# Stage B of a spectral mixer moved to 64x64 array tiles and the stages around it re-spaced, beside a dense feed-forward network

## Chip, cores, metric

One core of one Trainium2 chip. The metric is the device time of one execution in microseconds (us); lower is better. Every time below is the median of several executions, and all executions that are compared ran in the same (fast) state. "Granted clock" is the share of full TensorE clock that the profile's records show. The profiles are those of one execution each.

## The reference

```python
# x: (8, 3008, 256); filt_r, filt_i: (1505, 256); float32
X = np.fft.rfft(x, axis=1)
y = np.fft.irfft(X * (filt_r + 1j * filt_i)[None], n=3008, axis=1)
t = y.reshape(8 * 3008, 256)                       # 24064 tokens
out = (np.maximum(t @ w_gate, 0) * (t @ w_val)) @ w_out    # 256 -> 1536 -> 256
```

## The kernel before

A Fourier transform of length 3008 = 94 x 32 is done as matmuls. For each of the 8 batches there are these stages, which then feed the network (FFN):

- Stage A: transform of length 94. For batches 2 to 7 it goes in four *chunks* (j = 0 to 3): a load into one of three `XP` buffers, a *fold* of six operations on GpSimd, and a group of 16 small tiles on TensorE (`psF`). The result goes to DRAM (`Abuf`) and comes back as `at`.
- Stage B: transform of length 32 (`psX`), product with the filter on VectorE (`tt`, `uu`), inverse (`psD`). It goes to DRAM (`Dbuf`) and comes back as `dC`.
- Stage C: inverse of length 94 (`psY`), which gives the FFN's input `yT`.
- FFN: 47 blocks of 512 tokens with 12 *steps* each. A step is two `psV`, two `psG` and four `psO` matmuls. The stages of the next batches are hung on fixed step numbers between them, and TensorE takes everything in program order.

Stage A's chunks, and the schedule (cut):

```python
    def load_chunk(b, j):
        xp = XP[(4 * b + j) % 3]
        ...                       # six DMAs, issued by SyncE
    def fold_chunk(b, j):
        ...                       # six tensor_tensor on nc.gpsimd
    def tiled_a(b, j):
        ...                       # 16 tiles of 24 x 32 into four PSUM banks, two copies to asf by
        ...                       # ScalarE and two by VectorE, four DMAs to Abuf
    # the schedule, in FFN steps
        end = (b * S // W - 1) * NFT + C_AT[0] - 5
        sb0 = 19 if b == 1 else end - 30 | 1
        ...
            for j, (l, e) in enumerate(((-66, -41), (-60, -33), (-54, -27), (-40, -17))):
                at_step(sb0 + l, lambda b=b, j=j: load_chunk(b, j))
                at_step(sb0 + l + 1, lambda b=b, j=j: fold_chunk(b, j))
                at_step(sb0 + e, lambda b=b, j=j: tiled_a(b, j))
            at_step(sb0 + e + 4, lambda b=b: load_at_tiled(b))
        for i, f in enumerate(items_b(b)):
            at_step(sb0 + 2 * i, f)
        at_step(sb0 + 27, lambda b=b: load_d(b))
```

Stage B, one pair of groups (cut): each 128x128 matrix holds two 64x64 blocks on its diagonal.

```python
            for i in range(2):
                nc.tensor.matmul(psX[:, i], F2[:, g + i, :], at[:, g + i, :], start=True, stop=True)
            ...
            for i in range(2):
                nc.tensor.matmul(psD[:, i], I2t[:, g + i, :], tt[:, i], start=True, stop=False)
                nc.tensor.matmul(psD[:, i], I2u[:, g + i, :], uu[:, i], start=False, stop=True)
```

## Time and profile before

| | before |
|---|---|
| median, 3 runs before the prediction | 914.12 us (913.38 to 915.36) |
| span of the profiled execution | 911.3 us |
| TensorE busy | 98% |
| FFN starts at (first `psV` of the FFN) | 61.9 us |
| stage B between FFN steps, batches 1 to 7 | 55.0 us of TensorE |
| six fourth-chunk tile groups of stage A, each from the start of the last `psO` before it to the next `psV` | 1.46 us each |

The prediction shows the busy shares, the chain and the stage-B groups. From the page, the granted clock in 40 slices of the span (each digit is tenths; 9 is 90% or more). There is one dip, in the second slice:

```profile
PEclk9899999999999999999999999999999999999999
```

Columns are start (us), length (us), engine, line, operation, output<-input, count.

### The profile page before, as it was taken

To read this page: it belongs to the slowest core of one execution; us is meant where nothing else is said; L and a number is where in the kernel's file an instruction comes from. 1 tells how busy PE (TensorE), PEld (TensorE's weight loads), DVE (VectorE), ACT (ScalarE), POOL (GpSimd) and SP (SyncE) were. 2 spreads that over 40 slices of the span, in tenths; PEclk is the share of its full clock that TensorE was granted. 3 is DMA by queue.
4 is the path that set the end of the run, shared out by engine and by line. 5 is a ranking of instruction groups with operands and counts; after the bars stand their busy time and mean duration, and the time that the engine had idled before them with its cause. 6 is when DMAs were issued, how large, how long until landed. Compare 5 with 4: busy or idle time off the path is not lost.

```text
span 911.3 us, 18044 instructions
## 1 busy us (share of the span) xinstructions
PE 896.0 (98%) x6602; PEld 545.7 (60%) x6602; DVE 578.0 (63%) x875; ACT 500.8 (55%) x893; POOL 262.4 (29%) x181
## 2 busy tenths in 40 slices
PE   8799999999999999999999999999999999999997
PEld 3445665666655666556655566556665566666665
DVE  3737766568655775657755587555865567655553
ACT  4675555555555555555555555555555555555552
POOL 4340174405451074400844017440355300000000
PEclk9899999999999999999999999999999999999999
DMA  9996336444355345452353433525446242231111
GB/s 254 256 252 143 116 122 166 111 90 138 122 153 105 82 150 139 119 117 84 129 168 94 115 111 118 165 76 121 115 134 166 65 106 66 85 78 36 36 31 51
DMA packets 106138, 109.04 MB, mean 120 GB/s; under 512 B 9794, under 2 KB 87362, under 8 KB 105410
## 3 DMA queue, kind: packets, MB, share of 16 engines
q1 hardware_dynamic: 101222, 103.77, 40.7%
q0 software_dynamic: 4512, 3.90, 2.8%
q8 instruction: 52, 0.85, 0.4%
q14 instruction: 36, 0.29, 0.1%
q10 hardware_dynamic: 316, 0.22, 0.1%
HBM read 61.94 MB, written 49.81 MB: 123 GB/s over the span
## 4 chain that ended last, share of the span: by engine, by line
PE 95%; DMA 3%; SPq 0%; ACT 0%; POOL 0%; DVE 0%; issue 0%; ACTq 0%; POOLq 0%
PE psV L445 27%; PE psG L445 27%; PE psO L464 26%; PE psF L321 3%; PE psA L275 3%; PE psY L429 2%; PE psD L383 2%; PE psD L384 2%; PE psX L364 2%; DMA XF<-in_x_dram 1%; DMA Abuf<-asb 1%; DMA at<-Abuf 0%; DMA out_dram<-osb 0%; SPq L178 0%; SPq L478 0%
## 5 line engine op out<-in xcount | busy, mean ns | idle before, releaser
L450 DVE SCALAR_TENSOR_TENSOR prod<-psG,vsb 128x512 bf16<-128x512 f32 x564 | 390.0, 692 | 274.6 <-ACT vsb L448 265.6
L448 ACT CAST vsb<-psV 128x512 bf16<-128x512 f32 x564 | 332.0, 589 | 244.7 <-PE psV L445 206.4
L445 PE MATMUL psV<-yT,WvT 128*128 128x512 bf16 x1128 | 335.9, 379 | 0.9 <-ACT yT L434 0.7
L464 PE MATMUL psO<-WoT,prod 128*128 128x256 bf16 x2256 | 336.4, 273 | 0.0
L445 PE MATMUL psG<-yT,WgT 128*128 128x512 bf16 x1128 | 335.3, 379 | 0.0
L464 PEld LDWEIGHTS <-prod 128*128 128x128 bf16 x2256 | 220.7, 98 | 143.4
L445 PEld LDWEIGHTS <-WgT 128*128 128x128 bf16 x1128 | 110.0, 98 | 133.8 <-issue 0.5
L307 POOL TENSOR_TENSOR fold<-XP 128x1024 f32<-128x1024 f32 x24 | 56.4, 2351 | 404.5 <-DMA out_dram<-osb 170.9
L445 PEld LDWEIGHTS <-WvT 128*128 128x128 bf16 x1128 | 102.3, 98 | 33.1 <-issue 20.9
L386 ACT CAST dsb<-psD 128x512 bf16<-128x512 f32 x96 | 55.9, 588 | 51.7 <-PE psD L384 50.0
L367 DVE TENSOR_TENSOR tt<-psX,Ftr 128x512 bf16<-128x512 f32 x96 | 65.2, 682 | 4.2 <-PE psX L364 4.2
L470 ACT COPY osb<-psO 128x512 f32<-128x512 f32 x92 | 53.9, 586 | 22.7 <-PE psO L464 20.3
L373 DVE TENSOR_TENSOR uu<-psX,Fti 128x512 bf16<-128x512 f32 x90 | 61.3, 681 | 0.0
L308 POOL TENSOR_TENSOR XP<-XP 128x1024 f32<-128x1024 f32 x24 | 56.4, 2349 | 1.9
L384 PE MATMUL psD<-uu,I2u 128*128 128x256 bf16 x192 | 47.6, 276 | 0.6 <-POOL uu L371 0.6
L383 PE MATMUL psD<-tt,I2t 128*128 128x256 bf16 x192 | 47.9, 276 | 0.0
L328 ACT CAST asb<-psF 128x512 bf16<-128x512 f32 x48 | 25.8, 589 | 32.5 <-PE psF L321 32.5
L328 DVE CAST asb<-psF 128x512 bf16<-128x512 f32 x48 | 30.9, 686 | 17.3 <-PE psF L321 14.5
L364 PE MATMUL psX<-at,F 128*128 128x256 bf16 x192 | 37.8, 281 | 3.9 <-DMA at<-Abuf 3.9
L436 DVE CAST yT<-psY 128x512 bf16<-128x512 f32 x47 | 32.0, 681 | 12.9 <-PE psY L429 12.9
L434 ACT CAST yT<-psY 128x512 bf16<-128x512 f32 x47 | 27.5, 586 | 22.7 <-PE psY L429 22.6
L429 PE MATMUL psY<-M,dC 96*128 96x94 bf16 (+18 forms) x604 | 37.5, 198 | 0.0
(64 smaller groups left out, 439.9 us busy)
## 6 DMA issues: line engine op xcount, KB each, us to landing
dC<-Dbuf SPq DMA_DIRECT2D x64, 192.0 KB
XP<-in_x_dram SPq DMA_DIRECT2D x48, 256.0 KB
Dbuf<-dsb SPq DMA_DIRECT2D x31, 384.0 KB
XP<-in_x_dram SPq DMA_DIRECT2D x96, 96.0 KB
Abuf<-asb SPq DMA_DIRECT2D x96, 96.0 KB
at<-Abuf SPq DMA_DIRECT2D x48, 192.0 KB
out_dram<-osb SPq DMA_DIRECT2D x70, 94.0 KB
XF<-in_x_dram SPq DMA_DIRECT2D x12, 256.0 KB
```

Source lines behind the costliest of these rows:

```text
L307: tt(t, xp[:, 0:2], xp[:, 2:4], op=ALU.add)
L308: tt(xp[:, 2:4], xp[:, 0:2], xp[:, 2:4], op=ALU.subtract)
L328: copy(asf[:, :, q, :], banks[q])
L364: nc.tensor.matmul(psX[:, i], F2[:, g + i, :], at[:, g + i, :], start=True, stop=True)
L367: nc.vector.tensor_tensor(tt, psX, Ftr[:, g:g + 2, :], op=ALU.mult)
L373: nc.vector.tensor_tensor(uu, psX, Fti[:, g:g + 2, :], op=ALU.mult)
L383: nc.tensor.matmul(psD[:, i], I2t[:, g + i, :], tt[:, i], start=True, stop=False)
L384: nc.tensor.matmul(psD[:, i], I2u[:, g + i, :], uu[:, i], start=False, stop=True)
L445: nc.tensor.matmul(pt[:, :W], w[:, h, ft * 128:(ft + 1) * 128], yt[:, h, :], start=(h == 0), stop=(h == 1))
L448: nc.scalar.copy(vsb, psV[:, :W])
L450: nc.vector.scalar_tensor_tensor(prod, in0=psG[:, :W], scalar=0.0, in1=vsb, op0=ALU.max, op1=ALU.mult)
L464: nc.tensor.matmul(psO[:, t % 2], prods[ft][:, t * 128:(t + 1) * 128], WoT[:, ft, :], start=(ft == 0), stop=(ft == NFT - 1))
```

## The change

The intent: in a 128x128 matrix with two 64x64 blocks half of the array multiplies by zeros. On 64x64 tiles four blocks run side by side, so stage B's streaming time should halve. To pay for fewer mode switches, inverse and forward pieces are put into one excursion of 24 tile matmuls over four PSUM banks (two of `psX`, and `psv` and `psg` for `psD`), and the products go one to a step. The schedule is re-spaced for that. (Not shown in the cut: for batches 2 to 7 `at` comes in four loads instead of eight, and for batches 1 to 7 stage B's result goes to `Dbuf` in three stores instead of four.) Cut to its core:

```diff
+    def fwd(b, i, es=(0, 1)):
+        ...
+        for m in range(2):
+            for e in es:
+                for a in range(2):
+                    j = 12 * a + 2 * i + m
+                    nc.tensor.matmul(psXs[b, i, e][64 * a:64 * a + 64, m],
+                                     F2[64 * e:64 * e + 64, j, :],
+                                     ats[b][64 * e:64 * e + 64, j, :], start=True, stop=True,
+                                     tile_position=(64 * e, 64 * a))
+    def inv(b, i, tags=None, cuts=CUTS):
+        ...     # 16 matmuls with tile_position=(64 * a, 64 * e), into two banks
     def load_d(b, z0=0, z1=NZ):
         for z in range(z0, z1):
-            nc.sync.dma_start(dC, ...)                       # 96 rows
+            for e in range(2):
+                nc.sync.dma_start(dC[48 * e:48 * e + 48], ...)   # twice 48 rows
 # schedule
         if b == 1:
-                at_step(5, lambda c=c: load_at(1, c))
+                at_step(3, lambda c=c: load_at(1, c))
         else:
-            for j, (l, e) in enumerate(((-66, -41), (-60, -33), (-54, -27), (-40, -17))):
-                at_step(sb0 + l, ...)                        # sb0 = end - 30 | 1
+            for j, (l, e) in enumerate(((-104, -74), (-98, -69), (-92, -62), (-73, -57))):
+                at_step(end + l, ...)
-        for i, f in enumerate(items_b(b)):
-            at_step(sb0 + 2 * i, f)
-        at_step(sb0 + 27, lambda b=b: load_d(b))
+        for i, l in enumerate((-40, -35, -28, -23, -16, -11, -4)):
+            if i < 6:
+                at_step(end + l, lambda b=b, i=i: fwd(b, i))
+                for h in range(4):
+                    at_step(end + l + h, lambda b=b, i=i, h=h: product(b, i, h // 2, h % 2))
+            if i > 0:
+                at_step(end + l, lambda b=b, i=i: inv(b, i - 1, ("psv", "psg")))
+        at_step(end - 2, lambda b=b: load_d(b))
```

In the prologue (batch 0) the forward tiles run one bank at a time, with a filler matmul of 128 columns between them, as before; the forward matrices come by DMA instead of being placed by VectorE.

## The prediction

> **What bounds the kernel now.** I read the page's busy shares first, then the chain that ended last, then the TensorE timeline, and only then the waits.
>
> ```profile
> PE 896.0 (98%) x6602; PEld 545.7 (60%) x6602; DVE 578.0 (63%) x875; ACT 500.8 (55%) x893; POOL 262.4 (29%) x181
> PE 95%; DMA 3%; SPq 0%; ACT 0%; POOL 0%; DVE 0%; issue 0%; ACTq 0%; POOLq 0%
> L384 PE MATMUL psD<-uu,I2u 128*128 128x256 bf16 x192 | 47.6, 276 | 0.6 <-POOL uu L371 0.6
> L383 PE MATMUL psD<-tt,I2t 128*128 128x256 bf16 x192 | 47.9, 276 | 0.0
> L364 PE MATMUL psX<-at,F 128*128 128x256 bf16 x192 | 37.8, 281 | 3.9 <-DMA at<-Abuf 3.9
> ```
>
> TensorE is 95% of the chain, so the time is the sum of what TensorE issues, plus its few waits. VectorE and ScalarE have 37% and 45% to spare on average. The three stage-B groups have no idle before them except 3.9 and 0.6 us, both in the prologue. But their "busy" columns overstate: durations are latencies of overlapping matmuls. The true price is the distance from one start to the next:
>
> ```profile
> 83.11 0.60 PE L464 MATMUL psO<-WoT,prod 128*128 128x256 bf16 x4
> 83.54 0.38 PE L364 MATMUL psX<-at,F 128*128 128x256 bf16 x2
> 83.76 0.59 PE L445 MATMUL psV<-yT,WvT 128*128 128x512 bf16 x2
> 84.19 0.59 PE L445 MATMUL psG<-yT,WgT 128*128 128x512 bf16 x2
> 84.62 0.60 PE L464 MATMUL psO<-WoT,prod 128*128 128x256 bf16 x4
> 85.06 0.41 PE L429 MATMUL psY<-M,dC 96*128 96x10 bf16 x7
> ```
>
> Four 256-column matmuls take 83.54 - 83.11 = 0.43 us, so 0.109 us each; two of 512 columns take 0.43, so 0.216 each. An FFN step is 85.06 - 83.76 = 1.30 us. A batch's stage B is 24 forward and 48 inverse matmuls: 72 x 0.109 = 7.85 us. Seven of the eight batches run it between FFN steps (55 us); batch 0 runs it in the prologue.
>
> Is there a price for array tiles already in this kernel? Yes: the tiled stage A.
>
> ```profile
> 135.37 0.60 PE L464 MATMUL psO<-WoT,prod 128*128 128x256 bf16 x4
> 135.90 0.61 PE L321 MATMUL psF<-XP,WF 24*32 24x512 f32 x1
> ...
> 136.64 0.59 PE L321 MATMUL psF<-XP,WF 24*32 24x512 f32 x1
> 137.16 0.60 PE L445 MATMUL psV<-yT,WvT 128*128 128x512 bf16 x2
> ```
>
> The four psO should hand over at 135.37 + 0.43 = 135.80; the first tile starts at 135.90: entry costs about 0.09 us. The last tile matmul starts at 136.64 and streams 0.43 us (the fp32 psA matmuls follow one another by 0.43), so exit costs 0.52 - 0.43 = 0.09. Tiles of one row group start 7 ns apart, so they do run beside each other.
>
> **What the Trainium skill says.** "TensorEngine Tiling (Array Packing)", Key Properties: changing the tiling mode drains TensorE. The trace agrees: 0.09 us in and 0.09 out. The same page, Restrictions: column tiling turns fast weight load off. "TensorE: Matmul & The Clock Gate", LDWEIGHTS, gives columns / 1.2 ns for a weight load; for 64 columns an estimate of 53 ns. In psF, tiles' two passes start 0.43 or 0.45 us apart, which fits a later weight load (32 columns, 27 ns by that formula) mostly hidden behind the stream; no trace here has a 64-column one. The same page, the clock gate's two states: half clock after an idle window of about 3.4 us. The trace agrees: TensorE was idle from about 29.2 to 33.4 us in the prologue, and the mean granted clock was 0.52 from 31.5 to 38.5 us. I return to this below.
>
> **The change, part by part.**
> 1. Removed: 72 full-array matmuls per batch. They hold two 64x64 blocks on the diagonal and zeros beside them.
> 2. Added: 144 quarter-array matmuls of 256 columns per batch, in 36 quartets. If four tiles run beside each other, a quartet takes 0.109: 36 x 0.109 = 3.92 us. Four weight loads of 53 ns per quartet fit even if two by two they follow one another (0.106).
> 3. Added: mode switches. Before, forward and inverse pieces stood in the normal mode, no switch. Now there are seven excursions per batch: one forward only (2 quartets), five with forward and inverse (6), one inverse only (4). Each costs 0.09 in, 0.09 out and one exposed first weight load, 0.05: 0.23 us (an estimate). Seven: 1.6 us.
> 4. Sum per batch: 7.85 - (3.92 + 1.6) = 2.3 us; allowing 0.02 us stagger per excursion, 2.15. Times 7: 15 us.
> 5. VectorE and ScalarE do the same products (682 ns) and copies (588 ns) as before; they move. One product per step on four successive steps: VectorE needs 0.69 + 0.68 = 1.37 us per step against TensorE's 1.30. Four such steps fall behind by 0.28 us, but each excursion gives TensorE about 0.9 us more to do, and PSUM has two banks for each of psV and psG. The worst place is an excursion on step 11 of a block, where ScalarE queues osb (0.59), two psD copies (1.18) and then the next vsb (0.59). Counting from that block step's start: psD ready at about 2.4, vsb done at 4.1, prod at 4.8, while the psG bank is wanted by the step after next at about 5.2. It holds, with 0.3 to 0.4 us to spare; I book nothing.
> 6. Moved: batch 1's stage B starts at FFN step 11 instead of 19. This is the part I expect to cost time. What it needs is the load of its "at" tile:
>
> ```profile
> 61.40 0.30 SPq L280 DMA_DIRECT2D Abuf<-asb  x1
> 61.74 1.14 SPq L407 DMA_DIRECT2D dC<-Dbuf  x2
> 63.04 9.54 SPq L350 DMA_DIRECT2D at<-Abuf  x4
> 72.64 3.19 SPq L407 DMA_DIRECT2D dC<-Dbuf  x4
> ```
>
> The four loads (384 KB each) are issued until 72.6, and the issue of the last is drawn out: the queue is full. The DMA share is 1.19 from 72 to 76 us and 1.16 from 76 to 80, then 0.09. The queue still carries 512-byte packets until 80; counted in order behind the two dC loads (768 packets), the 3072 at packets end near 76.7, so the tile is usable at about 77. Before, the first forward matmul came at 83.54, 6 us later: no wait. In the changed kernel the loads are requested two steps earlier, but the order of the DMA queue in the built program is the same (two chunks of dC, at, four chunks of dC) and the bandwidth, not the request, limits it. Step 11's side work begins at about 72.3 (the step-12 psV starts at 72.73 in the old trace). So TensorE, which takes instructions in order, should wait about 4.6 us, once.
> 7. That wait is longer than 3.4 us, so it may cover a whole idle window and drop the clock to one half for some microseconds. If the windows run free, a 4.6 us gap covers one with chance (4.6 - 3.4) / 3.4 = 0.35, and then costs 2 to 3 us more (in the prologue half clock lasted 5 us after work resumed). On average 0.9 us.
> 8. Prologue: forward matrices now come by DMA, without the two VectorE placements (1.15 us busy), which lay beside loads. At its end, stage B gains perhaps 0.7 us on TensorE, but the first dC chunks landed near 60.0, when psY started at 60.6, so at most 0.5 shows. I book -0.4.
>
> Sum: 914.1 - 15.0 + 4.6 + 0.9 - 0.4 = 904.2; since the most likely single outcome has no clock drop, I say 903.5 us, -1.2%.
>
> **Rivals.** (a) No wait at step 11, because the loads land earlier than I count. For: the requests are two steps earlier and a half-microsecond shorter prologue helps. Against: the saturated queue until 80 us. It would make 898 to 899 us. (b) Free or nearly free switches, with weights fully hidden: 36 quartets only, a saving of 27 us and, with the wait, about 891. Against: the measured 0.09 each way in stage A. (c) Quartets limited by weight loads or by issue: if the four loads of 53 ns follow one another, a quartet takes 0.21 and the tiles save nothing; stage B would then cost 36 x 0.21 + 1.6 = 9.2 us, and the time would be about 928. Against: psF's sixteen tiles were issued 7 ns apart per row group. (d) VectorE becomes the bound in the four product steps: some 0.3 us for each of 42 product groups at worst, +10 us, 913. For: 1.37 against 1.30. Against: the ledger in point 5, and the 17.9 us that TensorE needs for twelve such steps against VectorE's 14.4 (12 x 0.69 + 0.68 + 8 x 0.68).
>
> **Range and chances.** The saving per batch is known to about 0.4 us (entry weight load and stagger), so 3 us over seven; the wait to 1.5; the clock drop is 0 or 2 to 3; (d) in part perhaps 3. Together 897 to 909. Faster by over 2% means below 895.8, which needs (a) and switches cheaper than measured: 0.1. Slower by over 2% needs (c) in full: 0.02. Within 2%: 0.88.
>
> **What would show it.** Right: no psX or psD group in the normal mode; start-to-start of the quartets near 0.109; from the start of the last psO before a full excursion to the next psV about 1.0 us (0.109 + 0.9); a TensorE wait of 4 to 5 us for "DMA at<-Abuf" near 72 us and none other of its kind; no new TensorE waits for ScalarE or VectorE. Wrong: excursions of 1.2 us or more (then (c)), psV or psG waiting for VectorE in steps after an excursion (then (d)), no wait near 72 us (then (a)).

## More of the kernel before

Now the fourth chunk of batch 2, in three timelines.

SyncE's issues first: the loads of `dC`, and later the first four of the six `XP` loads.

```profile
135.70 4.82 SPq L407 DMA_DIRECT2D dC<-Dbuf  x8
...
147.90 2.69 SPq L294 DMA_DIRECT2D XP<-in_x_dram  x4
```

The fold on GpSimd, its first and its last operation:

```profile
160.34 2.35 POOL L307 TENSOR_TENSOR fold<-XP 128x1024 f32<-128x1024 f32 x1 [12.77 <-DMA out_dram<-osb]
...
169.23 1.26 POOL L312 TENSOR_TENSOR XP<-XP 128x512 f32<-128x512 f32 x1
```

And TensorE, which uses it:

```profile
172.18 0.61 PE L321 MATMUL psF<-XP,WF 24*32 24x512 f32 x1
```

From the first request (147.90) to the end of the fold (169.23 + 1.26 = 170.49) are 22.6 us, and TensorE comes for it at 172.18. So this chain has only 1.7 us of slack in batch 2 (read in the same way, batches 3 to 7 have 3.5 to 6.8 us), and no view of TensorE's waits shows it, since a chain that is just in time makes no wait.

## The result, and the profile after

The changed kernel took 980.55 us (979.04 to 981.17, 4 runs) against 913.88 us (913.38 to 915.36, 4 runs) for the kernel before in the same rounds: ratio 1.072, interval 1.071 to 1.074. It is 7% slower. All ratios here are the mean time of one kernel's fast runs over that of the other's of the same rounds, so they are not quite the ratio of the medians quoted. The mean granted clock fell from 0.995 to 0.956.

From the page of the changed kernel: busy shares, granted clock, chain, and the stage-A tile group (count | busy us, mean ns | idle before, releaser).

```profile
PE 922.8 (94%) x7202; PEld 520.1 (53%) x7202; DVE 567.2 (58%) x873; ACT 497.9 (51%) x890; POOL 262.1 (27%) x181
...
PEclk9698999799998999989998999979999899999999
...
PE 87%; DMA 5%; POOL 4%; SPq 2%; issue 0%; ACT 0%; DVE 0%; POOLq 0%
...
L320 PE MATMUL psF<-XP,WF 24*32 24x512 f32 x384 | 47.5, 708 | 35.4 <-POOL XP L308 35.4
```

TensorE lost four points of busy share, and the chain now runs through DMA, GpSimd and SyncE for 11% of the span (3% before, almost all DMA). The clock line has eight dips instead of one. And the costly wait is at stage A's tiles, whose code the change did not touch. TensorE's waits (total us, times, longest):

```profile
PE psF L320 <- POOL XP L308: 35.4, 6, 7.9
PE psX L361 <- DMA at<-Abuf: 10.6, 2, 6.1
```

Six times, once for each of batches 2 to 7, TensorE waits for a fold. Here is batch 2 again, in the same three views. SyncE:

```profile
145.18 8.66 SPq L422 DMA_DIRECT2D dC<-Dbuf  x16
...
155.62 1.56 SPq L293 DMA_DIRECT2D XP<-in_x_dram  x4
```

GpSimd:

```profile
166.86 2.34 POOL L306 TENSOR_TENSOR fold<-XP 128x1024 f32<-128x1024 f32 x1 [14.27 <-DMA out_dram<-osb]
...
175.71 1.26 POOL L311 TENSOR_TENSOR XP<-XP 128x512 f32<-128x512 f32 x1
```

(The releaser in brackets is inferred. What the fold reads is the loads issued from 155.62 us on.) TensorE, with the idle time before and its releaser in brackets:

```profile
166.86 0.60 PE L480 MATMUL psO<-WoT,prod 128*128 128x256 bf16 x4
173.01 1.91 PE L320 MATMUL psF<-XP,WF 24*32 24x512 f32 x2 [5.55 <-POOL XP L308]
174.35 3.25 PE L320 MATMUL psF<-fold,WF 24*32 24x512 f32 x4
177.03 1.13 PE L320 MATMUL psF<-XP,WF 24*32 24x512 f32 x2
```

At this place the changed kernel is some 8 us behind on the clock (the FFN starts later, and batch 1 costs a wait, see below), so intervals have to be compared, not clock times. From the step that asks for the load to the first tile were 35.0 us before (137.16, that step's first `psV`, to 172.18). Now they would be 25.4 (141.99 to 167.4: the last `psO` starts at 167.19, and 0.11 of stream and 0.09 of entry follow). The request goes out 13.6 us after its step's start instead of 10.7, and from the request to the end of the fold are 21.4 us instead of 22.6. So the fold, which ended 1.7 us before TensorE could use it, now ends 9.6 us after (176.97). Over the six batches it is 7.8 to 11.9 us late. TensorE first waits 5.5 us for the fold's third operation, which gives the first of the four parts. Then the group itself stretches from 173.01 to 177.03 while the other parts come one by one from GpSimd. While TensorE was idle its clock was halved, from 172.63 for 10.24 us. The next `psV` came at 179.28, so the passage from the last `psO`'s start took 12.09 us against 1.46 before. The six fourth groups took 12.1, 12.3, 13.1, 12.4, 14.5 and 10.3 us. That is 65.9 us over 6 x 1.46. Of each half-clock stretch another 1.7 to 3.6 us lie behind the group, where the FFN runs at half speed: 16 us in sum, of which half, 8 us, is lost.

Stage B itself, from the same TensorE timeline, a full excursion in batch 1:

```profile
90.88 0.60 PE L480 MATMUL psO<-WoT,prod 128*128 128x256 bf16 x4
91.41 0.41 PE L361 MATMUL psX<-at,F 64*64 64x256 bf16 x8
91.66 0.28 PE L390 MATMUL psD<-tt,I2t 64*64 64x256 bf16 x4
91.77 0.28 PE L390 MATMUL psD<-uu,I2u 64*64 64x256 bf16 x4
...
92.19 0.60 PE L461 MATMUL psV<-yT,WvT 128*128 128x512 bf16 x2
```

The quartets of `psD` start 0.109 us apart. The last `psO` of four starts at 90.88 + 3 x 0.109 = 91.21, so entry costs 91.41 - 91.21 - 0.109 = 0.09, and the whole excursion adds 92.19 - 91.21 - 0.109 = 0.87 us. Over the trace the 35 full excursions have a median of 0.875, the seven forward-only ones 0.438, the seven inverse-only ones 0.657. A batch costs 5 x 0.875 + 0.438 + 0.657 = 5.47 us where it cost 7.86.

At batch 1, the foreseen wait:

```profile
75.12 0.59 PE L461 MATMUL psG<-yT,WgT 128*128 128x512 bf16 x2
81.86 0.64 PE L361 MATMUL psX<-at,F 64*64 64x256 bf16 x8 [6.14 <-DMA at<-Abuf]
```

The clock was at half from 80.47 for 6.83 us, until 87.30. The excursion took 6.88 us of TensorE instead of 0.44, and of the FFN behind it, from 82.43, 4.9 us ran at half clock: this cost 6.4 + 2.4 = 8.9 us (rounded after adding).

In the prologue, half clock lasted from 32.68 to 49.75 (17.07 us), against 31.75 to 38.58 (6.83 us) before, and the FFN starts at 64.24 instead of 61.91 us. This 2.3 us is uncertain: in the six profiles that have this prologue (this one and those of experiments 2, 3, 5, 8 and the first of 6) the FFN starts between 62.7 and 66.1 us, in the two with the old prologue at 61.9 and 62.9. One stretch of the changed kernel (us; then for PE, PEld, DVE, ACT and POOL busy time and count; granted clock; DMA share; GB/s) shows what is odd in it:

```profile
35.40:38.80 3.40, 3.40 (x34) 1.68 (x32) 3.40 (x7) 1.64 (x3) 1.04 (x1) 0.50 0.65 143
```

TensorE is busy all the time and its clock stays at half. (The profile models the ends of matmuls. By their columns, at the 0.43 us that 512 of them take at half clock, I estimate that something streams for 2.5 to 2.8 of each 3.4 us here.)

The account against the span of before, 979.2 - 911.3 = +67.9 us: fourth tile groups with the half clock after them +73.9, batch 1 +8.9, prologue +2.3, tiles 7 x (5.47 - 7.86) = -16.7. The sum is +68.4, 0.5 us over.

### The profile page after: what moved, and what is told of

Same layout as the page of the kernel before. It is cut to its first block, busy times and chain, and to the rows that moved or that the text cites. A ratio compares the mean times of both kernels' runs of the same rounds, so it can differ in the third digit from the quotient of the medians.

```text
span 979.2 us, 19294 instructions
## 1 busy us (share of the span) xinstructions
PE 922.8 (94%) x7202; PEld 520.1 (53%) x7202; DVE 567.2 (58%) x873; ACT 497.9 (51%) x890; POOL 262.1 (27%) x181
## 4 chain that ended last, share of the span: by engine, by line
PE 87%; DMA 5%; POOL 4%; SPq 2%; issue 0%; ACT 0%; DVE 0%; POOLq 0%
PE psV L461 24%; PE psO L480 24%; PE psG L461 23%; PE psF L320 5%; PE psA L274 3%; PE psD L390 2%; PE psY L445 2%; PE psX L361 2%; POOL XP L307 1%; POOL fold L306 1%; DMA at<-Abuf 1%; DMA out_dram<-osb 1%; DMA Abuf<-asb 1%; SPq L494 1%; DMA XP<-in_x_dram 1%; POOL XP L308 1%
## 5 line engine op out<-in xcount | busy, mean ns | idle before, releaser
L461 PE MATMUL psV<-yT,WvT 128*128 128x512 bf16 x1128 | 340.9, 384 | 0.5 <-ACT yT L450 0.5
L461 PE MATMUL psG<-yT,WgT 128*128 128x512 bf16 x1128 | 339.3, 383 | 0.0
L461 PEld LDWEIGHTS <-WvT 128*128 128x128 bf16 x1128 | 98.8, 98 | 47.0 <-issue 35.6
L320 PE MATMUL psF<-XP,WF 24*32 24x512 f32 x384 | 47.5, 708 | 35.4 <-POOL XP L308 35.4
L376 DVE TENSOR_TENSOR tt<-psX,Ftr 128x512 bf16<-128x512 f32 x96 | 65.3, 682 | 12.7 <-PE psX L361 12.6
L397 ACT CAST dsb<-psD 128x512 bf16<-128x512 f32 x96 | 51.5, 589 | 25.4 <-PE psD L390 25.3
L320 PE MATMUL psF<-fold,WF 24*32 24x512 f32 x384 | 52.7, 714 | 0.3 <-POOL fold L309 0.3
L445 PEld LDWEIGHTS <-dC 96*128 96x128 bf16 x604 | 34.6, 97 | 3.6 <-issue 1.0
```

The costliest lines, as they stand in the source:

```text
L320: nc.tensor.matmul(banks[q][32 * c:32 * c + 32], WF[r:r + 24, c, :], fold[b, j][c][r:r + 24], start=True, stop=True, tile_position=(r, 32 ...
L376: nc.vector.tensor_tensor(p, psX, filt, op=ALU.mult)
L397: nc.scalar.copy(dsb[:, a, o:o + 2, :], psD[a])
L445: nc.tensor.matmul(psY[:, o:o + w], dCs[b, n2 // 4][:, n2 % 4, h * 128:(h + 1) * 128], M1[:, n1:n1 + w], start=True, stop=True)
L461: nc.tensor.matmul(pt[:, :W], w[:, h, ft * 128:(ft + 1) * 128], yt[:, h, :], start=(h == 0), stop=(h == 1))
```

## The experiments

My theory after reading the traces was that stage B's tiles gain what I had said, and that the loss is the schedule of the fourth chunk, made worse by the clock. The rivals: the tiles themselves bring the loss (clock, contention for the memories, PSUM banks), or batch 1 and the prologue, which delay all that follows. All the kernels below gave correct results. Ratios are against the kernel before of the same rounds, with four runs of each kernel and seven of the kernel before, which ran at 913.7 to 913.9 us.

**1. Stage A's new spacing alone, in the kernel before.** Stage B, its matrices and its loads are untouched; the four pairs of offsets give the steps of the changed kernel.

```diff
-            for j, (l, e) in enumerate(((-66, -41), (-60, -33), (-54, -27), (-40, -17))):
+            for j, (l, e) in enumerate(((-74, -44), (-68, -39), (-62, -32), (-43, -27))):
```

> The kernel before, with its full-array stage B untouched, but with the four stage-A chunks of each batch at the steps of the changed kernel (tiles at end-74, -69, -62, -57 instead of -71, -63, -57, -47). Theory (the moved stage A is the loss: the fourth chunk's load stands behind the dC loads in the DMA issue queue, its fold comes late, TensorE waits and its clock halves): slower by 35 to 55 us, 950 to 970, with TensorE waits of about 6 us at the fourth tiled stage A of six batches. It should be less than in the changed kernel (about 72 us there), because eight dC loads instead of sixteen stand ahead. Rival (the 64x64 tiles are the loss): 914, no wait.

Measured: 961.3 us (960.1 to 962.4), ratio 1.052 (1.050 to 1.053), granted clock 0.976. Without one 64x64 tile the re-spacing costs 47 us. The fourth tile groups take 4.4, 8.5, 9.4, 8.1, 7.3 and 8.0 us. Five of the six come with a half clock of 6.8 us, one with 3.4. So the spacing alone is enough for 47 us. The fold is 2.8 to 6.9 us late. Batch 3's first tile:

```profile
276.17 1.11 PE L321 MATMUL psF<-XP,WF 24*32 24x512 f32 x2 [1.88 <-POOL XP L309]
```

It is worse in the changed kernel (65.9 against 36.8 us in the tile groups). There the request for the chunk goes out 11.9 to 14.7 us after its step's start, here 6.6 to 11.2 and in the kernel before 7.6 to 10.7, with the same 20 to 23 us from request to end of fold in all three. What stands one step ahead of it in the changed kernel is twice as many `dC` loads, issued over 8.66 us instead of 4.82 (batch 2).

**2. The chunk's load ahead of the `dC` loads.** In the changed kernel, at step end - 2 of batch b, the first tile group of batch b + 1 (which frees the buffer) and the fourth load come before the load of `dC`.

```diff
+        if b + 1 < B:
+            at_step(end - 2, lambda b=b: tiled_a(b + 1, 0))
+            at_step(end - 2, lambda b=b: load_chunk(b + 1, 3))
         at_step(end - 2, lambda b=b: load_d(b))
```

> The changed kernel, with only the order of two things in the same FFN step turned round: the fourth chunk's load is issued before the dC loads of the batch before. Theory (issue order): the six waits at the fourth tiled stage A and their half-clock stretches go, about 72 us: 907 to 912. Rival (GpSimd has too little time between the tiles even with the data there): the wait shrinks by less than half, over 940. Rival (tiles are the loss): 980.

Measured: 950.24 us (949.1 to 955.8), ratio 1.041 (1.038 to 1.044). I had expected all of it to go; 30 us went. Every fourth tile group now takes 1.45 to 1.47 us: the fold is in time. But the waits have moved. TensorE's waits in this kernel, and its SyncE timeline:

```profile
PE psY L445 <- DMA dC<-Dbuf: 30.9, 8, 5.5
```

```profile
146.64 12.87 SPq L422 DMA_DIRECT2D dC<-Dbuf  x16
```

Now `dC` stands behind the chunk. Its issue begins 1.5 us later, in a run whose FFN began 1.6 us earlier, and is drawn out over 12.9 instead of 8.7 us (probably because the chunk's transfer is under way), and stage C waits 4.6 to 5.5 us six times, each time with a half clock of 3.4 to 6.8 us after it. The two loads are wanted at the same time, and whichever is second is late. The order of issue is part of the cause; the other part, which experiment 5 tests, is that both must wait until that step.

**3. Batch 1 later.** Its first two excursions at steps 15 and 19 instead of 11 and 16.

```diff
-        for i, l in enumerate((-40, -35, -28, -23, -16, -11, -4)):
+        for i, l in enumerate((-36, -32, -28, -23, -16, -11, -4) if b == 1
+                             else (-40, -35, -28, -23, -16, -11, -4)):
```

> The changed kernel, with batch 1's stage B starting at FFN step 15 instead of 11 (second excursion at 19). Theory (that batch waits for its at tile, limited by the DMA queue, not by the request): the 6.1 us wait falls to about 1 us and the half clock after it (80.5 to 87.3 us) goes: 7 to 8 us less, 972 to 974. If the wait moves along with the start: 980.

Measured: 976.65 us (975.8 to 978.5), ratio 1.068 (1.067 to 1.070): 3.9 us below the changed kernel, about half of what I had expected. The wait at 75 us and the half clock after it are gone, but in the profiled execution the FFN began at 66.1 us (64.2 in the changed kernel), and step 20 brought a new wait of 1.6 us, of `psY` for a product of VectorE, probably because the excursion at 19 is next to it. The six fourth tile groups also took 77.6 us in this execution, against 74.7. Steps 14 and 18 (experiment 6) avoid that wait but for 0.3 us.

**4. Fuller fillers in the prologue.** To see whether tile work keeps the clock low, the filler between batch 0's forward tiles is made four times as long.

```diff
         if i < 9:
-            warm(1, 128)
+            warm(1, 512)
```

> The changed kernel, with the filler matmul in each of the first nine prologue stage-B pieces 512 columns wide instead of 128. Theory (in the prologue the half clock lasts to 49.7 us instead of 38.6 because tiled work with drains and waits leaves TensorE too little active): full clock returns before 43.7 us and the FFN starts about 2 us earlier, 978 to 979. Rival (tiled matmuls themselves do not release the clock, or the FFN start is set by the DMA of dC): no change, 980.5.

Measured: 985.42 us (980.7 to 987.8), ratio 1.078. The half clock lasted longer, 20.48 us from 32.95, and the FFN began at 68.2. So my expectation fell: with a 512-column filler of about half of each forward tile-and-filler passage, a clock that is already at half did not come back for 20 us.

**5. A fourth `XP` buffer.** This takes away what makes the load wait: with one buffer per chunk the fourth load need not wait for the first tile group and goes out at step end - 86, 12 steps before the `dC` of the batch ahead. The buffer is paid for with one of five output buffers (with five it did not fit: 77 KB wanted per partition, 76.1 left).

```diff
-        xp = XP[(4 * b + j) % 3]
+        xp = XP[j]                                    # in load_chunk and fold_chunk
-            osb = fs.tile([128, 2, D], FP32, tag="osb", bufs=5)
+            osb = fs.tile([128, 2, D], FP32, tag="osb", bufs=4)
-        for i in range(3):
+        for i in range(4):                            # in clear_chunks
-            for j, (l, e) in enumerate(((-104, -74), (-98, -69), (-92, -62), (-73, -57))):
+            for j, (l, e) in enumerate(((-104, -74), (-98, -69), (-92, -62), (-86, -57))):
```

> The changed kernel with a fourth XP buffer (paid for with one osb buffer less), so that the fourth chunk needs not wait for the first tile's buffer and is requested 13 steps earlier, ahead of the last Dbuf write and the dC loads. Theory (the fourth chunk's late load is the whole of the stage-A loss, and in the run with the loads turned round the wait only moved to dC behind the same queue): no wait at the fourth tile and none for dC, about 72 us less: 906 to 912. Rival (GpSimd is too late for the earlier deadline even with its data there, since the fold needs 10.2 us and must wait for the first tiles): waits of several us stay at the fourth tile and the time stays over 925.

Measured: 910.80 us (910.3 to 911.3), ratio 0.997 (0.995 to 0.998). It takes 70 us off the changed kernel, and nothing of stage B was touched. The tile groups are back at 1.28 to 1.62 us, and no half clock follows after batch 1. The same place of batch 2 in TensorE's timeline:

```profile
168.10 0.61 PE L320 MATMUL psF<-XP,WF 24*32 24x512 f32 x1
...
169.27 0.39 PE L461 MATMUL psV<-yT,WvT 128*128 128x512 bf16 x1
```

The tiles are as before in this run, the fold ended at 162.9, and the loss is gone: this settles where 70 us came from.

**6. The best version.** The fourth buffer, with batch 1's first excursions at steps 14 and 18; and that once more with full-array fillers before batch 0's first forward tile.

```diff
+        for i, l in enumerate((-37, -33, -28, -23, -16, -11, -4) if b == 1 else ...):
```

> Four XP buffers, and batch 1's stage B from FFN steps 14 and 18 on instead of 11 and 16. Expected: 7 us less than with four XP buffers alone, 900 to 904. If the wait for at moves along: no gain.

```diff
         warm(6)
+    warm(18)
     place_own()
```

> All three repairs together. Theory A of the fill: 2 us less than without it, 897 to 902, faster than the kernel before by 1.3 to 1.8%. Theory B: no better than without it.

Measured: 906.12 us (902.8 to 908.4), ratio 0.991 (0.989 to 0.994), and 904.56 us (902.4 to 910.5), ratio 0.992 (0.988 to 0.996). Both are faster than the kernel before, by 0.8 to 0.9%, which is the "same" at a limit of 2%; the two are not told apart, and both lie above what I had expected. In the second one's profile TensorE comes to batch 1's first tiles 2.1 us too early, instead of 6.5. Its seven batches of stage B show the same 0.438, 0.875 and 0.657 us, and the FFN starts at 64.2, still 2.3 us late. The account: 16.7 - 2.3 - 2.1 - 0.8 (one `psY` that waits for `dC`, at 577 us) = 11.5 us; the spans of the two profiled executions differ by 911.3 - 900.6 = 10.7, so 0.8 us is not accounted for.

**7. Fillers in the prologue of the changed kernel alone.** Only `warm(18)` is added, so that TensorE isn't idle before the first forward tile. It tells whether the idle time or the tiles halve the clock there.

> The changed kernel with 18 more filler matmuls (3.9 us) in the prologue's idle stretch before the first forward tile. Theory A (the clock is halved there by the idle stretch alone, and tiled work then cannot bring it back): it is never halved in the prologue, FFN starts at 61.5 to 62.5 instead of 64.2: 977 to 979. Theory B (array-tiled work with fillers counts as too little activity in itself): the clock halves some microseconds later, during the tiled work, and the FFN start does not improve.

Measured: 982.16 us (979.3 to 983.5), ratio 1.074. The idle time before the first tile is filled and the clock is not halved at 32 us any more. But it is halved at 39.22 us for 6.83 us, in the middle of tile work, after a stretch (35.4 to 38.8 us) in which TensorE was busy for 2.35 of 3.40 us. The kernel before keeps its full clock through and after a stretch with less, 1.86 of 3.40 us (42.2 to 45.6). So the idle time starts the long half clock of the changed kernel, but among tiles the clock can fall without it. The time of the whole is not better.

**8. Full-array matmuls in place of the waits.** 44 matmuls of 512 columns (about 9.5 us) before each fourth tile group of the changed kernel: the wait stays, but TensorE works in it. What the time falls by is the clock's share of the loss.

```diff
+                if j == 3:
+                    at_step(end + e, lambda: busy(44))
                 at_step(end + e, lambda b=b, j=j: tiled_a(b, j))
```

> The changed kernel with 44 useless full-array matmuls of 512 columns (9.5 us) in front of each fourth tiled stage A, where TensorE waits some 10 us for GpSimd. They run inside the wait, so the wait itself stays; what they can take away is the half clock. Theory (72 us at these six places are about 6 x 9 us of waiting and 6 x 3 us of half clock): full clock after each, 15 to 22 us less, 959 to 965. Rival (the half-clock stretches hide in the waits, or the fillers push the tiles back as much as they save): 978 to 983.

Measured: 969.06 us (966.6 to 971.9), ratio 1.060. The half clock after the waits is gone but for one stretch of 3.4 us, the mean granted clock is 0.984, and the time falls by 11.5 us. That is less than I had expected. The passages through the fourth tile groups, fillers included, still sum to 73.2 us in its profile (74.7 in the changed kernel), so most of what is gained is the FFN's part behind them, for which the trace gave 8 us. The clock's share of the loss is thus about 8 to 12 us; the waits themselves are the rest, about 62 to 66.

**9. The share of full-array work among tiles.** On the best version, batch 0's forward tiles for both halves go with the inverse into one excursion (half as many switches); once with six fillers of 512 columns per excursion and once with two of 128.

```diff
+        for i in range(6):
+            fwd(0, i)
+            if i >= 2:
+                inv(0, i - 2, cuts=cuts)
+            for e in range(2):
+                ...
+                amid(2 * i + e)                       # the filler
-            warm(1, 128)
+            warm(3, 512)                              # the first of the two only
```

> All three repairs, and in the prologue both halves of a forward piece and the inverse of two pieces before in one excursion (six excursions instead of some twenty), with six full-array filler matmuls of 512 columns after each (1.3 us). Theory (the half clock comes from the share of time in which full-array work runs; 49% at half clock in the run with wider fillers was not enough, about 60% may be): clock full from 33 us on and the FFN start 1 to 3 us earlier, 901 to 904. Rival (tiled work in a stretch halves the clock whatever stands beside it, or the dC transfer sets the FFN start): 904 to 907.

> As the one before, with the small fillers (two of 128 columns per excursion) left as they are. Theory (share of full-array work): the clock is halved for two or more windows in the prologue; 903 to 907. If the number of mode switches was what lowered the activity, the clock stays full here as well and the time equals that of the other or is less.

Measured: 907.35 us (905.6 to 909.5), ratio 0.993, and 906.46 us (903.0 to 908.8), ratio 0.992. One stretch of each, in the columns of the stretch shown above, first with six long fillers:

```profile
35.40:38.80 3.40, 3.25 (x42) 1.53 (x42) 3.40 (x7) 1.23 (x3) 1.13 (x2) 1.00 0.87 175
```

then with two short ones:

```profile
35.40:38.80 3.40, 1.75 (x34) 1.13 (x36) 3.40 (x7) 1.84 (x4) 1.18 (x2) 0.85 0.73 167
```

With long fillers the clock stays full all through the prologue; with short ones it is at half from 37.81 for 10.24 us. The number of switches is the same, so it isn't their number. The long fillers raise TensorE's busy time (3.25 against 1.75 of 3.40 us) as well as the share of full-array work, so these two runs alone don't tell which of them the clock goes by; the stretch of the changed kernel shown further up (busy 3.40 of 3.40 us, mostly tiles, clock 0.50) says that it isn't busy time alone. And the full clock shows no gain: with it the FFN starts at 65.3, after 3.1 us of waiting for `dC` (and 3.4 us of half clock follow); with the half clock at 63.2, after 0.4. These are single executions, and the start of the FFN differs by up to 3.4 us between executions of one prologue (above). What the first of them does show is that with the clock repaired its prologue's end was set by the landing of `dC`, not by TensorE.

Three kernels were built and not run: the fourth buffer beside five output buffers, the `dC` loads as one DMA each (its access pattern can't be described in three dimensions), and the first experiment with a fourth buffer (77 KB wanted, 69.1 left; with four output buffers still 75 KB). The last would have been the cleanest control; it doesn't fit since it lacks the room that the halved matrices of stage B give (9 KB per partition).

## Why the prediction was wrong, point by point

**What bounds the kernel; price of the tiles (points 1 to 4): right.** Quartets 0.109 us, entry 0.09, exit 0.10 (the last quartet starts at 91.98, the `psV` at 92.19), 0.875 for a full excursion against 6 x 0.109 + 0.23 = 0.88 predicted. Per batch 2.39 us saved, against 2.15 to 2.3; in seven batches 16.7 against 15. One figure in it was wrong and cost nothing: a 64-column weight load took 110 to 111 ns (mean) in the profile of the changed kernel, not the estimated 53. The profile before could have warned: stage A's 32-column loads took 102 ns there, not the 27 that I read into them, and a 128-column load 98. The quartets start 0.109 us apart all the same, so the loads of a quartet overlap.

**VectorE and ScalarE (point 5, rival d): right.** From the start of the FFN on, TensorE's waits for either come to no more than 0.5 us, and that is the first block's `yT`. Rivals (b) and (c) are out with the quartets, and (a) with the wait.

**Batch 1 (points 6 and 7): mechanism right, sizes too small.** The wait was 6.1 us, not 4.6. TensorE came for the tile at 75.7, not 72.3, mostly since the prologue ended later; the tile came at 81.9, not 77. The half clock, which I had booked with a chance of 0.35, did come: 8.9 us in place of 5.5. The reckoning behind that chance, that a window of 3.4 us must be idle throughout, does not hold. In the profile of before, TensorE's last matmul ended at 29.43, and the clock was halved 2.3 us later, at 31.75. In experiment 1 it was halved at 277.01 after the pause of 1.88 us shown there and sparse tiles, and in experiment 2 around all six waits of 4.6 to 5.5 us. In the last run of experiment 9, this wait was followed by half clock from 82.18:

```profile
81.56 0.41 PE L361 MATMUL psX<-at,F 64*64 64x256 bf16 x8 [2.25 <-DMA dC<-Dbuf]
```

A pause of 2.0 us in the second run of experiment 6 was not followed by one, so the length alone doesn't decide.

**Prologue (point 8): wrong in sign, small.** +2.3 us in place of -0.4, with the uncertainty said above. I credited tiles there. In the changed kernel TensorE came late, after a half clock of 17 us (it did not wait for `dC` at the prologue's end); with the clock repaired, it waits up to 3.1 us for `dC` (experiment 9).

**What was moved (point 6): this step failed, and it is nearly the whole of the miss.** It named batch 1's earlier stage B as what the re-spacing costs, and the last part of the prediction asked for a wait on `at` near 72 us "and none other of its kind". Re-spacing stage A of batches 2 to 7 was in the diff and I priced it at nothing. It cost 73.9 us, and the time is 77 us over the 903.5 that I gave. The profile of before held most of what was needed. The chunk's chain had 1.7 us of slack in batch 2 and 3.5 to 6.8 in the others, 4.5 in the mean. The diff moves the tile step 10 steps ahead (from end - 47 to end - 57) and the load step only 3 (from end - 70 to end - 73). Seven steps of 1.30 us are 9.1 us, so the fold should be late by an estimated 9.1 - 4.5 = 4.6 us in the mean; in experiment 1, which does only this, it is 2.8 to 6.9 us late. The diff also puts the load one step behind the `dC` of the batch ahead, where it stood 5 to 7 steps behind, and makes that load sixteen issues instead of eight. In the changed kernel the request went out 4.8 us later after its step, in the mean (13.6 against 8.8), and the fold was 7.8 to 11.9 us late.

**The clock's weight.** I had thought of the half clock as an accident of one wait. It came with all seven long waits; the stretches are 6.83, 10.24 or 13.65 us long, all multiples of 3.41 us. Experiment 8 puts it at 8 to 12 of the 74 us.

**Range.** The range 897 to 909 took in the tiles, batch 1 and rival (d), all terms that I had priced; it had no room for a term that I had not looked for. The repaired version at 904.56 us is about where the prediction was, but by other sums: more from the tiles, less from a wait, more lost in the prologue. That they meet is luck.

**Open.** How much full-array work per window holds the clock: six of 512 columns per excursion did, two of 128 did not, and fillers over about half of each forward tile-and-filler passage did not bring it back for 20 us once lost. The limit was not sought, nor was busy time kept the same between the two. And the fourth buffer in the kernel before could not be tried.

## What to carry to other kernels

When a change re-spaces a software pipeline, go through every chain that has a new deadline, also those whose code is unchanged: add request, place in the issuing engine's order, transfer and processing from the old trace, and hold the sum against the new interval. A stage that shows no waits may have little slack, and not the same each time (here 1.7 to 6.8 us). Where two loads were wanted at the same step here, changing their order took away 30 us and moved the wait to the other; another buffer, which let one go out earlier, took it away.

## What the Trainium skill lacked or had wrong

- "TensorE: Matmul & The Clock Gate", Part 1, has the full clock come back "After ≥1 busy SHORT window (~3.4µs sustained)". Here TensorE was busy, as the profile counts it, for all of 35.4 to 42.2 us, with 64x64 tiles and short fillers, and the granted clock stayed at 0.50 until 49.75; in experiment 7 it fell to half during tile work with TensorE busy for 2.35 of the 3.40 us before. The page doesn't say whether tile work counts for less than full-array work; these numbers suggest that it does, and don't show it.
- The same page, LDWEIGHTS, has the time of a weight load go with its columns, and has no figure for tiles narrower than 128 columns. Measured durations: 98 ns for 128 columns, 110 to 111 for 64 columns of a 64x64 tile, 102 for 32 columns of stage A's tiles in the kernel before.
- "TensorEngine Tiling (Array Packing)", Key Properties, says that a mode change drains TensorE and gives no number. Measured here: 0.09 us in and 0.09 (stage A) to 0.10 us (stage B) out between matmuls of 256 or 512 columns, and 0.22 us per excursion in all (0.875 - 6 x 0.109).
- "Perfetto Trace Analysis", Per-instruction lifecycle, has the issuing sequencer free for the next instruction only when a DMA is issued, and gives no number for what that does to a load further back. Here the fourth chunk's request came at 155.62 us, after sixteen `dC` loads that took from 145.18 to 153.84 to issue, 13.6 us after its step began; before, with eight loads ahead by some steps, 10.7 us after.
